# Reloading stored sums between transposing loads, and moving four additions behind the last sums, at the end of a gated feed-forward kernel

## The chip, the core and the metric

The kernel runs on one core of one Trainium2 chip. The metric is the device time of one execution in microseconds (us). The kernel before took 540.11 us as the median of three runs (540.02 to 540.7). The profile comes from one further execution, which took 539.99 us; its span from the first to the last instruction is 538.2 us, so 1.79 us lie around the span. The engines are PE (matrix products), DVE (elementwise, two inputs), ACT (copies, casts, the gelu), POOL (elementwise) and SP, which here only issues DMAs. ACT issues a few DMAs too.

## The reference

```python
def reference(x, w_gate, w_up, w_down):      # x 1x2048x1024, w_gate and w_up 1024x3584, w_down 3584x1024, bf16
    g = jnp.einsum("bsd,df->bsf", x, w_gate)
    u = jnp.einsum("bsd,df->bsf", x, w_up)
    h = _gelu(g) * u
    return jnp.einsum("bsf,fd->bsd", h, w_down)
```

## The kernel before, in words

The 2048 rows are taken in two passes of 1024 rows, each of two halves of 512 rows. In each pass the gate and up products run first, with h left in the on-chip memory, and then the down product (function `down`). All three products use Strassen's scheme in Winograd's form: a 2x2 block product is made of seven products of sums of blocks instead of eight, and the blocks of the result are sums of these products. In `down` the four blocks of the result ("quadrants" of the pass) are two halves of the rows by two halves of the columns.

In the second pass `down` goes one level deeper for one of its products (function `apart`): its result comes out transposed, as 16-bit planes written to DRAM (`pt0` to `pt3`), and is read back with transposing DMA loads. This concerns two quadrants, which the code numbers 0 and 1: quadrant 0 is read back by eight transposing loads issued from ACT, quadrant 1 by eight issued from SP (`turn_back`, the DMA at line 745). Two loads, n and n + 4, make one piece of 128 rows; there are four pieces for each quadrant. ACT puts the planes of a piece together into 32-bit numbers (`join`, line 750, 128x1024 16-bit elements).

What is then done with them, line by line:

- Quadrant 0 completes four pieces of the **first pass's** output. For these the sums of the first pass had been stored to DRAM (`ud`, line 949). `fetch_u3(i)` reloads the sum of piece i (line 757, 128x512 32-bit, 256 KB, a DMA on SP's queue). `put_0(i)` joins piece i of quadrant 0 on ACT into a buffer `gt`, adds the reloaded sum on DVE (line 121, the helper through which every DVE operation is recorded, output `st`), and stores the result (line 850, on SP's queue).
- Quadrant 1 completes four pieces of the second pass. `join_1(i)` joins piece i on ACT into the buffer `turned[1]`, which the end of `down` adds to four finished banks of products (line 946).

The last stretch of `down` (lines 937 to 957) makes what the code calls the products 7 and 3. For t from 0 to 13 one step is taken from the agenda, and then four matmuls of product 7 (`rows(e, q73[t][0], ...)`) are issued; with a lag of three steps six of the fourteen quadruples of product 3 run between them, and the other 32 matmuls at the very end, ordered by piece, with a final addition and store after each piece. The operands of step t are made by `make73(j)`: three DVE operations of 128x512 (outputs `q`, lines 670 to 672: `s3`, `t3` for product 7, and `s4` for product 3) and one cast on ACT (`tb`, line 677 for j below 8 and line 133 from 8 on). "Last sums" in the change's name are the ones that `make73` makes for j = 10 to 13.

In the second `down` the order on every engine is that in which the code calls the operations (`manual_schedule` holds all five engines there). The agenda is a table by step: `at(last, step, what, *args)` enters a call, `step()` makes the calls entered for the current step, in the order in which they were entered. Steps 66 to 79 are the fourteen turns of t in the last stretch. `make73(10)` to `make73(13)` stand at the steps 70, 71, 72 and 73 and come first in their steps, since they were entered earlier. SP works through its DMAs in the order of issue; an issue that has to wait holds all later ones.

Buffers for `u3`, `gt`, `q`, `tb`, `st` come from one pool of 36 slots (`kpool`): a new tile takes over a slot whose last reader has to be done. Moving a call therefore changes which slot each later tile gets, and so the waits.

Of the kernel before, what the change touches and what calls it, by code (L numbers as in the profile page):

```python
# [10 lines left out]
def kernel(  # L11
# [794 lines left out]
    def at(last, step, what, *args):  # L806
        agenda.setdefault((last, int(step)), []).append((what, args))
# [24 lines left out]
        at(1, 52 + n // 2, turn_back, 0, n)  # L832
        at(1, 59 + n, turn_back, 1, n)
    for i in range(NS):
        at(1, 66 + i, fetch_u3, i)
        at(1, (70, 72, 74, 76)[i], put_0, i)
        at(1, (71, 73, 75, 77)[i], join_1, i)
    moves = [(c, ko) for ko in range(KH) for c in range(2)]
    moves += [(c, ko) for c in (1, 0) for ko in range(KH, NKB)]
    sa = {}  # L840
# [483 lines left out]
```

## Time and profile before

| what | value |
| --- | --- |
| median of three runs | 540.11 us (540.02 to 540.7) |
| profiled execution, its span | 539.99 us, 538.2 us |
| PE busy | 529.5 us, 98% of the span |
| DVE busy | 404.0 us, 75% |
| ACT busy | 302.2 us, 56% |
| POOL busy | 268.3 us, 50% |
| granted PE clock | 1.0 in every slice |
| last PE matmul ends, last DVE operation ends | 534.75 us, 535.47 us |
| PE busy from 520 to 539 us of the span | 10.94 of 19 us |

All times within the profile are microseconds from the start of the span. In the timeline a row is: start, duration, engine, line, operation, output<-input, number of instructions merged; in square brackets the idle time of the engine ahead of the row and what ended it. `u<-ud` is the reload of a stored sum, `w<-pt` a transposing load, `gt<-w` the join of quadrant 0, `w<-w` at line 750 the join of quadrant 1, `st<-gt,u` the addition of `put_0`, `st<-bank,...` the final additions. "SPq" stands for the issuing of DMAs on SP. The chain of work that ended last is followed back from the last instruction, at each step to what released it.

### The profile page before, as it was taken

The page shows a single profiled execution, that of the slowest core. Times are in us where ns is not written, and L with a number is a line of the kernel's source. Part 1 is how long each engine was busy: PE and PEld are TensorE (multiplying, and loading weights), DVE is VectorE, ACT ScalarE, POOL GpSimd, SP SyncE. Part 2 cuts the span into 40 slices and gives each one's busy share as a digit, 9 for nine tenths or more (in the row PEclk, how much of TensorE's full clock was granted, in tenths as well). Part 3 has the DMA queues.
Part 4 walks back from the last instruction along what each step waited for, and adds up shares of the span by engine and source line. Part 5 has one row for each costly group of instructions (what it writes and reads, how often), then busy time and mean ns, then how long its engine had stood idle before and what let it go on. Part 6 is the DMA issues. An engine that isn't in the chain of part 4 may idle for free.

```text
span 538.2 us, 7762 instructions
## 1 busy us (share of the span) xinstructions
PE 529.5 (98%) x2375; PEld 374.2 (70%) x2375; DVE 404.0 (75%) x645; ACT 302.2 (56%) x544; POOL 268.3 (50%) x259
## 2 busy tenths in 40 slices
PE   9999999999999999999999999999999999999986
PEld 5568686868676774688877686866767764778754
DVE  2988768787777786749699887658576599789837
ACT  2557686868586841015576776666666621181742
POOL 1179977979797960000004989694896700000000
PEclk9999999999999999999999999999999999999999
DMA  9795218685777699999897999947363599599854
GB/s 244 162 240 174 80 60 292 197 293 197 234 233 247 205 377 381 369 316 246 227 293 215 302 315 355 250 117 197 88 186 118 198 362 345 160 319 320 182 129 146
DMA packets 141161, 126.09 MB, mean 234 GB/s; under 512 B 31680, under 2 KB 119232, under 8 KB 141120
## 3 DMA queue, kind: packets, MB, share of 16 engines
q1 hardware_dynamic: 136768, 124.55, 75.5%
q10 hardware_dynamic: 4352, 1.05, 1.1%
q8 instruction: 19, 0.31, 0.2%
q14 instruction: 22, 0.18, 0.1%
HBM read 86.38 MB, written 31.06 MB: 218 GB/s over the span
## 4 chain that ended last, share of the span: by engine, by line
PE 91%; DVE 3%; SPq 3%; DMA 1%; issue 1%; ACT 1%; DVEq 0%; ACTq 0%
PE bank L145 91%; DVE q L121 2%; SPq L745 2%; DMA w<-in_w_up_dram 1%; DVE xT L121 1%; DMA u<-ud 1%; ACT s L875 0%; SPq L995 0%; SPq L757 0%; DVE st L121 0%; ACT u L138 0%; SPq L662 0%; SPq L1014 0%; DVEq L121 0%; ACTq L138 0%
## 5 line engine op out<-in xcount | busy, mean ns | idle before, releaser
L124 POOL TENSOR_TENSOR s<-w 128x512 fp32r<-128x512 bf16 x102 | 117.5, 1170 | 49.6 <-DMA w<-in_w_gate_dram 35.5
L145 PE MATMUL bank<-t,s 128*128 128x512 f32 x528 | 126.3, 392 | 0.0
L145 PEld LDWEIGHTS bank<-t,s 128*128 128x128 f32 x528 | 99.1, 188 | 21.6 <-POOL s L124 0.3
L145 PE MATMUL bank<-xT,w 128*128 128x512 bf16 (+1 forms) x504 | 110.4, 376 | 0.1
L145 PEld LDWEIGHTS <-w 128*128 128x128 bf16 x504 | 47.7, 98 | 58.3 <-issue 4.2
L213 ACT ACTIVATE g<-sum 128x512 f32<-128x512 f32 x81 | 51.5, 636 | 59.8 <-DVE sum L121 57.8
L138 ACT COPY p<-bank 128x512 f32<-128x512 f32 x98 | 55.1, 590 | 47.3 <-PE bank L145 47.3
L121 DVE TENSOR_TENSOR hT<-g,bank 128x512 bf16<-128x512 f32 x72 | 48.9, 687 | 18.0 <-ACT g L213 12.4
L145 PE MATMUL bank<-q 128*128 128x512 f32 x224 | 57.4, 394 | 4.1 <-DVE q L121 3.9
L124 POOL TENSOR_TENSOR s<-w,s 128x512 fp32r<-128x512 bf16 x50 | 57.8, 1174 | 0.4
L124 POOL TENSOR_TENSOR s<-s,w 128x512 fp32r<-128x512 f32 x50 | 57.4, 1168 | 0.2
L121 DVE TENSOR_TENSOR bank<-bank,p 128x512 f32<-128x512 f32 x74 | 51.3, 695 | 5.9 <-PE bank L145 5.3
L145 PE MATMUL bank<-t,sa 128*128 128x512 f32 x216 | 54.9, 397 | 0.0
L145 PE MATMUL bank<-tb,s 128*128 128x512 f32 x216 | 54.3, 394 | 0.0
L199 POOL COPY seen<-t 128x1 f32<-128x1 f32 x2 | 0.4, 184 | 107.2 <-DVE t L121 107.2
L145 PEld LDWEIGHTS bank<-q 128*128 128x128 f32 x224 | 41.8, 188 | 15.0 <-DVE q L121 5.7
L145 PEld LDWEIGHTS bank<-t,sa 128*128 128x128 f32 x216 | 40.6, 188 | 9.1
L145 PEld LDWEIGHTS bank<-tb,s 128*128 128x128 f32 x216 | 40.5, 188 | 9.0 <-POOL s L124 0.3
L121 DVE TENSOR_TENSOR sum<-bank,p 128x512 f32<-128x512 f32 x54 | 37.0, 685 | 12.8 <-PE bank L145 11.7
L138 ACT COPY u<-bank 128x512 f32<-128x512 f32 x62 | 35.4, 595 | 17.4 <-PE bank L145 13.7
L133 ACT CAST tb<-raw 128x512 fp32r<-128x512 bf16 x20 | 12.4, 627 | 36.5 <-DMA raw<-in_w_down_dram 30.1
L133 ACT CAST sa<-w 128x512 fp32r<-128x512 bf16 x54 | 30.7, 616 | 2.7 <-DMA out_dram<-st 2.7
(121 smaller groups left out, 733.2 us busy)
## 6 DMA issues: line engine op xcount, KB each, us to landing
raw<-in_w_down_dram SPq DMA_DIRECT2D x72, 256.0 KB, 5.5
w<-in_w_gate_dram SPq DMA_DIRECT2D x27, 512.0 KB, 4.6
w<-in_w_up_dram SPq DMA_DIRECT2D x27, 512.0 KB, 5.9
td<-m SPq DMA_DIRECT2D x11, 768.0 KB, 5.3
q<-td SPq DMA_DIRECT2D x28, 256.0 KB, 5.2
pd<-xT SPq DMA_DIRECT2D x10, 512.0 KB, 5.7
w<-td SPq DMA_DIRECT2D x5, 1024.0 KB, 7.7
p<-pd SPq DMA_DIRECT2D x20, 256.0 KB, 4.8
```

The source lines that it names most:

```text
L121: nc.vector.tensor_tensor(out=out, in0=a, in1=b, op=op)
L124: nc.gpsimd.tensor_tensor(out=out, in0=a, in1=b, op=op)
L133: nc.scalar.copy(out=t, in_=src)
L138: nc.scalar.copy(out=t, in_=ps)
L145: nc.tensor.matmul(ps, lhsT=lhs, rhs=rhs, start=start, stop=stop, skip_group_check=True)
L199: nc.gpsimd.tensor_copy(out=seen, in_=tile[:, :1].bitcast(f32))
L213: nc.scalar.activation(g, src, ACT.Gelu_apprx_tanh)
L745: queue.dma_start_transpose(out=turned["tp", quad][:, i, half], in_=pt[2 * quad + half][:, i * P : (i + 1) * P])
```

## The change

```diff
     for n in range(2 * NS):
         at(1, 52 + n // 2, turn_back, 0, n)
         at(1, 59 + n, turn_back, 1, n)
     for i in range(NS):
-        at(1, 66 + i, fetch_u3, i)
-        at(1, (70, 72, 74, 76)[i], put_0, i)
-        at(1, (71, 73, 75, 77)[i], join_1, i)
+        at(1, 61 + i, fetch_u3, i)
+        at(1, 75 + i, put_0, i)
+        at(1, 71 + i, join_1, i)
```

NS is 4. No operation is added or removed. On SP's queue the four reloads move from behind the eighth transposing load of quadrant 1 to the places behind its third, fourth, fifth and sixth. On ACT the four joins of quadrant 1, which alternated with those of quadrant 0, come first, between the casts of `make73(11)` to `make73(13)` and behind them, and the four joins of quadrant 0 follow as the last work of ACT. On DVE the four additions of `put_0`, of which one stood behind `make73(10)`, one behind `make73(12)` and two behind `make73(13)`, all stand behind `make73(13)`, ahead of the final additions to the banks. PE's and POOL's orders are the same. The slots that `u3`, `gt` and the later `q` and `tb` tiles take over are other ones.

## The prediction

> **What bounds the kernel now.** I read the chain of work that ended last first, since PE's 98% is a mean over the span. PE holds it until the last 35 us; from there it leaves PE.
>
> ```profile
> 511.82 1.26 SPq L745
> 513.13 2.06 SPq L745
> 515.23 1.26 SPq L745
> 516.59 0.52 SPq L757
> 518.15 3.13 DMA u<-ud
> ...
> 526.22 8.54 PE bank L145 x36
> 534.78 0.69 DVE st L121
> ```
>
> SP's row of transposing loads, then the reloads, then DVE's sums, then PE, then the last addition, which ends at 535.47. The timeline of DVE and of PE tells what stands behind this:
>
> ```profile
> 508.82 0.69 DVE L121 TENSOR_TENSOR q<-hL,q 128x512 fp32r<-128x512 bf16 x1
> 520.06 0.69 DVE L121 TENSOR_TENSOR st<-gt,u 128x512 bf16<-128x512 f32 x1 [10.56 <-DMA u<-ud]
> 520.67 0.68 DVE L121 TENSOR_TENSOR q<-hT 128x512 fp32r<-128x512 bf16 x1
> ```
>
> ```profile
> 517.96 1.99 PE L145 MATMUL bank<-q 128*128 128x512 f32 x8
> 522.01 1.20 PE L145 MATMUL bank<-q 128*128 128x512 f32 x4 [2.07 <-DVE q L121]
> 523.81 1.21 PE L145 MATMUL bank<-q 128*128 128x512 f32 x4 [0.60 <-DVE q L121]
> 526.22 1.20 PE L145 MATMUL bank<-q 128*128 128x512 f32 x4 [1.19 <-DVE q L121]
> ```
>
> DVE stands 10.56 us on the first addition of put_0, whose reload is the ninth DMA behind the transposing loads. The nine sums of make73(11) to make73(13) are queued behind it, and PE starts the last three quadruples of product 7 late. Three waits, 3.86 us in all; by starts it is more. A quadruple takes 0.93 us when nothing waits (516.10 to 517.02), so the eight matmuls at 517.96 would be followed at 519.82. The real starts are 522.01, 523.81, 526.22 and 527.25: lost are 2.19 + 0.87 + 1.48 + 0.10 = **4.64 us**. That is all that can be had here.
>
> **The change, part by part.**
>
> *DVE's wait goes.* Behind 508.82 the nine sums follow at DVE's pace of 0.60 us. Owing to the other slots, one sum of make73(9) waits in the changed program for a product 7 matmul that ends at 507.9 instead of for one three quadruples earlier; that puts DVE back by 0.9 us. The sums end near 508.82 + 0.69 + 0.9 + 9 x 0.60 = 515.8. PE needs the first of them at 519.82, so it has 4 us of cover, and PE's last matmul ends at 534.76 - 4.64 = 530.1. I found no other new wait on DVE or PE that comes later than its engine's own work.
>
> *SP's row gets longer.* The eight transposing loads begin at 503.49, 506.74, 507.92, 509.22, 510.52, 511.82, 513.13 and 515.23; the first reload now stands behind the third. A reload behind a transposing load costs SP 0.52 us and 0.10 of semaphore and gaps (516.49 to 517.11, plus 0.05); a transposing load behind a copy took 1.14 and 1.16 instead of 1.26 (503.49, 506.74). So each of the four reloads adds about 0.55. Without the one long issue (2.06 instead of 1.26 at 513.13) the eighth began at 514.4; with four reloads at 516.6, with a long issue again at 517.4. The buffers of the reloads cost no wait: the matmuls and the sum that they wait for ended by 501.7. Queued behind the first reload are five transposing loads, behind the last two, and then only the output stores, which cannot start before 522.
>
> *When the eighth has landed.* Every load of quadrant 1 has these times to landing, and issue times beside them:
>
> ```profile
> L745 SPq DMA_TRANSPOSE w<-pt x8: 1136/1258/2062, 503.5 to 515.2; - x8
> DMA to landing us min/median/max: 2.6/4.6/6.3
> ```
>
> The second row spans both queues; SP's eight alone have a median of 2.7 and a longest of 4.2, those issued from ACT beside heavy loading 5.9. A transposing load with a 256 KB reload 1.2 us ahead of it is not in this stretch; the bounds are 2.6 and 6.0. I take 3.1, nearest to SP's own rows, since the seventh stands between the last reload and the eighth. The eighth has landed at 516.6 + 3.1 = **519.7**, 1.8 us later than now (515.23 + 2.7 = 517.9).
>
> *ACT and DVE behind it.* This is what is late next. In the changed order the join of piece 3 of quadrant 1 waits for the eighth load, and the four joins of quadrant 0, whose data has lain ready since about 503, stand behind it. A join follows a join after 1.065 us and takes 1.16: the last ends at 519.7 + 4 x 1.065 + 1.16 = 525.1. DVE's fourth addition starts there; twelve final additions follow, at 0.60 each, as they ran in
>
> ```profile
> 530.29 2.47 DVE L121 TENSOR_TENSOR st<-bank,w 128x512 bf16<-128x512 f32 x4
> ```
>
> The last starts at 525.15 + 12 x 0.60 = 532.35 and takes 0.69: **533.04**. PE, done at 530.1, would allow 530.8; so the end passes from PE to the chain SP, landing, ACT, DVE, and 2.2 of the 4.64 us are given back. Each 1 us by which the eighth load lands later moves the end by 1 us; at 522.1 nothing is won.
>
> *The stores.* Sixteen stores follow DVE at 0.60 us; SP issues one in 0.33, landing 1.7. The 2.73 us from the last addition to the end of the span stay.
>
> **Sum.** 535.47 - 533.04 = 2.43 us off 539.99 gives 537.56; the median of the runs lies 0.12 above the profiled execution, so 537.7.
>
> **A rule to weigh.** The reloads put 1 MB of reads among the transposing loads. The Trainium skill, "DMA: Bandwidth & Descriptors", section "Latency and other measured facts", gives the memory's access latency as 0.2 us on average and 2 us at high load. If that is the state they make, each landing is 1.8 us longer than SP's 2.7, an estimate from that page: the eighth lands at 521.1 and the sum is 539.1. The trace has both: 2.7 alone, 5.9 beside other loads at a DMA share above 1.0; the share here, from 507 to 519, is 0.41 to 0.82.
>
> **Rivals.**
>
> 1. *PE stays the bound.* If SP issues the reloads in the gaps (DMA share 0.33 at 510 to 512) and the eighth lands by 517.5, the additions are through when PE is: 530.83 instead of 535.47, so 535.5. For it: without the long issue the eighth would begin at 514.4 and need 2.6. Against it: each reload has a measured 0.37 to 0.52 of issue on the same queue. 0.06.
>
> 2. *Crowding.* The transposing loads land with the median of all sixteen, 4.6, not 3.1: end 1.5 later, 539.2; with the 5.9 of ACT's, 540.5. For it: the load issued at 511.82 took 4.2 with nothing but transposing loads about, and a stretch of 512 to 514 shows a DMA share of 0.91 at 128 GB/s. Against: a reload of 262144 bytes each 1.9 us (one reload and one transposing load on SP) is 138 GB/s, against 349 at 519 to 521, where the reloads run alone. 0.14.
>
> 3. *Slower: the queue changes between copies and transposing loads one after the other.* If a load of one kind starts only when the last of the other kind has landed, eight changes lie between the third load of quadrant 1 and the seventh. At 2.7 and 3.3 us each (the landings of a transposing load and of a reload) this puts the eighth at 536 and the time at 554. The place is SP's row; slower than now begins at a landing of 522.1, slower by over 0.2% at 523.3, that is at 0.45 us for each change. For it: nothing shows such a close mix here. Against: the four 128 KB weight loads issued right behind the first transposing load landed in 2.3 to 2.7, and the second, issued 0.06 after the last of them, in 2.8, so two changes cost nothing; in the first pass two transposing loads between copies (268.52, 271.74) landed in 4.3 and 3.1. At a mild 0.6 for each change the time is 542.5. 0.08. The Trainium skill, same page, "Rules for kernel authors", says that a transpose next to ordinary DMAs needs nothing; by that, this rival falls.
>
> That the change does not do what it says (a reload held by its buffer, so that SP stands) has no support: their last readers are done at least 7 us before.
>
> **How the numbers follow.** Forecast 537.7 with 0.72 (its own range, landing 2.6 to 4.0 with and without a long issue: 537.2 to 538.9). A change of under 0.2%, 1.1 us, is about what a measurement of this kernel can't tell from none. Faster than 539.0: 0.72 + 0.06 + 0.04 of crowding = 0.82. Within 0.2%: 0.10. Slower: 0.08. The range 536.4 to 539.6 leaves out the PE bound below, and above it the slower rival and the upper part of crowding, 0.18 in all.
>
> **What would show it.** Right: no idle of DVE ahead of a st<-gt,u with releaser "DMA u<-ud" of 10 us; PE without gaps from 484 to 530; idle ahead of ACT's w<-w joins with releaser "DMA w<-pt"; the four gt joins last on ACT, ending near 525; DVE without a gap for the final twelve additions and the chain's end through ACT and SP instead of PE. Wrong: a PE wait on q behind 518; a transposing load between reloads that lands after 4 us or more or whose issue takes over 2 us; a last addition that waits for PE, which would mean rival 1.

## The result, and the profile after

| | before | after |
| --- | --- | --- |
| median of ten runs each | 541.28 us (539.02 to 542.89) | 539.06 us (538.75 to 540.3) |
| ratio after / before | | 0.9967 (95% interval 0.9951 to 0.9983) |
| a second measurement, 12 runs against 28 | 542.02 us | 540.16 us, ratio 0.9965 (0.9948 to 0.9983) |
| profiled execution, its span | 539.99, 538.2 us | 540.3, 538.5 us |

The change gains 0.33%, 1.8 us, with an interval of 0.9 to 2.7; the ratio is that of the means, and the medians lie 2.2 us apart. The forecast was 2.43 us, a ratio of 0.9955, and a time of 537.7 us, which none of the ten runs reached.

The two spans don't show this gain: they begin the last stretch at different times. The first transposing load of quadrant 1 ("the first load" below) is issued at 503.49 in the profile before and at 504.41 after. I therefore count from the first load. The last addition ends 31.98 us behind it before, 31.37 after; another profile of each gives 31.75 (first load at 505.54) and 30.95 (504.82). So the stage itself gains 0.4 to 1.0 us, where 2.43 were forecast.

SP's row after the change, from the timeline (start, duration):

```profile
510.19 0.52 SPq L757 DMA_DIRECT2D u<-ud  x1
510.75 1.12 SPq L745 DMA_TRANSPOSE w<-pt  x1
...
513.77 1.58 SPq L757 DMA_DIRECT2D u<-ud  x1
515.39 1.12 SPq L745 DMA_TRANSPOSE w<-pt  x1
516.61 0.52 SPq L757 DMA_DIRECT2D u<-ud  x1
517.18 2.43 SPq L745 DMA_TRANSPOSE w<-pt  x2
```

A reload costs 0.52 and the transposing load behind it 1.12, as forecast; one issue is long again (1.58). What these loads set in motion is seen on ACT and on DVE:

```profile
517.32 1.17 ACT L750 COPY w<-w 128x1024 uint16<-128x1024 uint16 x1 [6.52 <-DMA w<-pt]
518.39 0.62 ACT L133 CAST tb<-raw 128x512 fp32r<-128x512 bf16 x1
518.97 1.17 ACT L750 COPY w<-w 128x1024 uint16<-128x1024 uint16 x1
520.05 0.61 ACT L133 CAST tb<-raw 128x512 fp32r<-128x512 bf16 x1
521.34 2.24 ACT L750 COPY w<-w 128x1024 uint16<-128x1024 uint16 x2 [0.68 <-DMA w<-pt]
523.49 4.39 ACT L750 COPY gt<-w 128x1024 uint16<-128x1024 uint16 x4
```

```profile
515.96 0.68 DVE L121 TENSOR_TENSOR q<-hL,q 128x512 fp32r<-128x512 bf16 x1
524.69 0.69 DVE L121 TENSOR_TENSOR st<-gt,u 128x512 bf16<-128x512 f32 x1 [8.05 <-ACT gt L750]
...
535.10 0.68 DVE L121 TENSOR_TENSOR st<-bank,u 128x512 bf16<-128x512 f32 x1
```

The 10.56 us of waiting ahead of DVE's sums are gone: the sums now run through and end at 516.64. DVE still stands for 9.2 us, 8.05 and then three times 0.4, but later, and on ACT's joins of quadrant 0 instead of a reload. ACT begins with the joins of quadrant 1 at 517.32, when the fifth load lands (issued at 512.55, landed in 4.7), and the last of them starts 18.0 us behind the first load, where the forecast says 16.2. PE runs product 7 without a gap:

```profile
517.82 1.10 PE L145 MATMUL bank<-xT,q 128*128 128x512 f32 x4
518.75 4.71 PE L145 MATMUL bank<-q 128*128 128x512 f32 x20
```

The chain that ended last no longer goes through PE at its end:

```profile
517.18 4.14 DMA w<-pt
...
523.58 4.31 ACT gt L750 x4
...
528.52 2.48 DVE st L121 x4
...
531.60 4.18 DVE st L121 x7
```

The seventh load's landing (4.14 us), ACT, DVE: the passage that was forecast, 1.8 us later than forecast.

Landings of SP's eight transposing loads, in us from the start of the issue; the reloads stand ahead of loads 4 to 7 in the changed kernel and in `e11`. Two of the rows are of kernels that start with more warm-up matmuls (`e8`, `e11`); they are explained with their experiments.

| kernel | 1 | 2 | 3 | 4 | 5 | 6 | 7 | 8 |
| --- | --- | --- | --- | --- | --- | --- | --- | --- |
| before | 2.6 | 2.8 | 2.8 | 2.7 | 2.7 | 4.2 | 3.6 | 2.7 |
| after | 2.7 | 2.8 | 2.7 | 3.9 | 4.7 | 3.6 | 4.1 | 3.5 |
| after, second profile (`e5_after_again`) | 3.3 | 2.6 | 2.7 | 3.7 | 4.9 | 4.2 | 3.4 | 2.9 |
| `e1_late_adds` | 2.5 | 2.7 | 2.7 | 2.7 | 4.5 | 3.9 | 3.3 | 2.6 |
| `e8_shifted_program` | 2.4 | 3.5 | 2.7 | 2.5 | 2.6 | 2.7 | 2.6 | 2.8 |
| `e11_after_shifted` | 3.6 | 3.3 | 2.8 | 3.9 | 4.0 | 3.9 | 4.1 | 3.4 |

### The profile page after: what moved, and what is told of

The parts are those of the page before. It is cut to its first block, busy times and chain, and to the rows that moved or that the text cites. A ratio compares the mean times of both kernels' runs of the same rounds, so it can differ in the third digit from the quotient of the medians.

```text
span 538.5 us, 7762 instructions
## 1 busy us (share of the span) xinstructions
PE 528.5 (98%) x2375; PEld 374.9 (70%) x2375; DVE 404.4 (75%) x645; ACT 302.0 (56%) x544; POOL 268.4 (50%) x259
## 4 chain that ended last, share of the span: by engine, by line
PE 89%; DMA 4%; DVE 3%; ACT 2%; issue 1%; SPq 0%; ACTq 0%; DVEq 0%
PE bank L145 88%; DMA w<-pt 2%; DVE q L121 2%; DVE st L121 1%; DMA raw<-in_w_down_dram 1%; ACT gt L750 1%; DMA q<-td 1%; PE bank L1057 1%; PE bank L1002 1%; ACT s L875 0%; ACT xT L733 0%; SPq L662 0%; DVE xT L121 0%; ACTq L1319 0%; ACT u L138 0%
## 5 line engine op out<-in xcount | busy, mean ns | idle before, releaser
L121 DVE TENSOR_TENSOR hT<-g,bank 128x512 bf16<-128x512 f32 x72 | 49.0, 687 | 17.6 <-ACT g L213 11.9
L133 ACT CAST tb<-raw 128x512 fp32r<-128x512 bf16 x20 | 12.3, 624 | 37.3 <-DMA raw<-in_w_down_dram 29.0
```

Source lines behind the costliest of these rows:

```text
L121: nc.vector.tensor_tensor(out=out, in0=a, in1=b, op=op)
L133: nc.scalar.copy(out=t, in_=src)
```

## The experiments

**Theory A**: the reloads among the transposing loads make quadrant 1 late, and the second part of the change, which puts all of ACT's and DVE's ready work behind quadrant 1, exposes that. **Rival B**: the reloads cost nothing there; the joins are late for a reason that both kernels share. **Rival C**: the late additions are of use only with the early reloads.

In every diff the minus lines are the changed kernel's. All times in the stage are in us, counted from the first load of that kernel's own profile. That is the right zero where the chain to the end runs through these loads. Where PE is the bound (`e4`, `e10`) it is not quite: in the kernels with 7 warm-up matmuls in which no sum holds PE, PE's last matmul ends 25.3 to 26.9 us behind the first load, so these two compare with the others only to within about 1.5 us. All rows but the first two are of one profile each:

| kernel | last join of quadrant 1 starts | last addition ends | ratio to before |
| --- | --- | --- | --- |
| before, two profiles | 23.15, 22.93 | 31.98, 31.75 | |
| after, two profiles | 18.00, 17.58 | 31.37, 30.95 | 0.9967, 0.9965 |
| `e1_late_adds` | 15.77 | 29.12 | 0.9898 (0.9869 to 0.9927) |
| `e2_early_reloads` | 21.10 | 29.09 | 0.9923 (0.9896 to 0.995) |
| `e3_reloads_ahead` | 15.56 | 28.93 | 0.9917 (0.9888 to 0.9947) |
| `e4_adds_in_gap` | 15.52 | 26.30 | 0.9872 (0.9845 to 0.99) |
| `e6_split_reloads` | 19.15 | 32.51 | 0.9999 (0.9979 to 1.002) |
| `e7_half_reloads` | 16.5 | 29.94 | 0.9936 (0.9913 to 0.9959) |
| `e8_shifted_program` | 14.24 | 27.61 | one execution |
| `e10_joins_in_gap` | 14.53 | 27.12 | 0.9904 (0.9877 to 0.9932) |
| `e11_after_shifted` | 17.62 | 31.00 | one execution |
| `e12_half_shift` | 14.34 | 27.70 | one execution |

### The second part alone: e1_late_adds

```diff
-        at(1, 61 + i, fetch_u3, i)
+        at(1, 66 + i, fetch_u3, i)
```

> Only the second part of the change: the additions and joins of quadrant 0 late as in the changed kernel, the four reloads behind the eighth transposing load as before. Theory A (the reloads among the transposing loads delay the joins of quadrant 1, and with them the end): the eighth load is issued 11.7 us behind the first and the last join of quadrant 1 starts 14.5 us behind it instead of 18.0; the last addition ends 27.9 us behind the first load instead of 31.4, so the time is about 3.5 us below the changed kernel, 4 us below the kernel before. Rival B (the reloads cost the row nothing; the changed kernel fell short because its execution lost time ahead of the changed part, and the row of transposing loads is as slow without them): last addition again 31 us behind the first load, time within 0.7 us of the changed kernel. Rival C (the late additions need the reloads early): DVE waits for a reload behind the joins, last addition later than 31.4.

The reloads go back behind the eighth load, the additions stay late. SP and ACT:

```profile
506.03 9.51 SPq L745 DMA_TRANSPOSE w<-pt  x7
515.64 1.95 SPq L757 DMA_DIRECT2D u<-ud  x4
```

```profile
514.30 1.17 ACT L750 COPY w<-w 128x1024 uint16<-128x1024 uint16 x1 [6.16 <-DMA w<-pt]
...
517.49 2.23 ACT L750 COPY w<-w 128x1024 uint16<-128x1024 uint16 x2
519.62 4.39 ACT L750 COPY gt<-w 128x1024 uint16<-128x1024 uint16 x4
```

The first join starts 11.5 us behind the first load instead of 12.9, no later join waits, and the reloads, issued last, are there before ACT has made `gt`. The stage is 1.8 to 2.2 us shorter than with both parts. Rivals B and C fall. The end is later than theory A had it, since the fifth load still took 4.5 us; `e8` and `e12` look into that.

### The first part alone: e2_early_reloads

```diff
-        at(1, 75 + i, put_0, i)
-        at(1, 71 + i, join_1, i)
+        at(1, (70, 72, 74, 76)[i], put_0, i)
+        at(1, (71, 73, 75, 77)[i], join_1, i)
```

> Only the first part of the change: the four reloads among the transposing loads, the additions and joins of quadrant 0 where they were before, alternating with those of quadrant 1. Theory A: the transposing loads land as late as in the changed kernel (fifth 12.9 us, seventh 16.9 us behind the first), but two joins of quadrant 0 are done before and between those of quadrant 1, so the last join starts about 20.5 us behind the first load with no other join behind it; DVE has done all four additions of put_0 by 21.2 and ends 28.4 behind the first load: 3 us below the changed kernel. Rival B: nothing to gain from the order of the joins, within 0.7 us of the changed kernel. Rival C (the second part was needed to free DVE): make73(13) stands behind an addition that waits for a join, PE waits on q by 1 us or more, slower than the changed kernel.

DVE, with the additions where they were before:

```profile
514.42 0.69 DVE L121 TENSOR_TENSOR st<-gt,u 128x512 bf16<-128x512 f32 x1 [2.26 <-DMA u<-ud]
...
521.34 0.69 DVE L121 TENSOR_TENSOR st<-gt,u 128x512 bf16<-128x512 f32 x1 [2.62 <-ACT gt L750]
...
526.14 0.69 DVE L121 TENSOR_TENSOR st<-gt,u 128x512 bf16<-128x512 f32 x1 [1.44 <-ACT gt L750]
```

Of the 10.56 us of waiting 2.26 are left, and PE waits for none of the sums. The transposing loads behind reloads land as late as in the changed kernel (loads 4 to 8: 3.6, 5.4, 4.7, 3.4, 3.0), but the joins of quadrant 0 alternate with those of quadrant 1 and fill ACT's time between landings: its last join begins at 526.02 with nothing behind it, and the end is 29.09. **Either part alone takes away the wait that PE felt, and each alone gains about 2 us more in the stage than both.**

### Reloads ahead of all transposing loads: e3_reloads_ahead

```diff
-        at(1, 61 + i, fetch_u3, i)
+        at(1, 58, fetch_u3, i)
```

> The changed kernel with its four reloads ahead of the first transposing load of quadrant 1 (agenda step 58 instead of 61 to 64), where SP stands idle for 3 us; joins and additions as in the changed kernel. Theory A: the row of transposing loads is as short as before (eighth issued 11.7 us behind the first), the last join of quadrant 1 starts 14.5 us behind the first load; the first load itself comes 0 to 1 us later; time 2.5 to 3.5 us below the changed kernel. Rival B: time within 0.7 us of the changed kernel.

```profile
499.63 3.67 SPq L757 DMA_DIRECT2D u<-ud  x4
504.72 1.16 SPq L745 DMA_TRANSPOSE w<-pt  x1
507.97 9.29 SPq L745 DMA_TRANSPOSE w<-pt  x7
```

With the reloads ahead, on SP's free time, the row of loads is as short as in `e1`, and so is the stage (28.93). It is the reloads' place among the loads that costs, not that they are made.

### Ready work into ACT's wait: e4_adds_in_gap

```diff
-        at(1, 61 + i, fetch_u3, i)
-        at(1, 75 + i, put_0, i)
-        at(1, 71 + i, join_1, i)
+        at(1, 58, fetch_u3, i)
+        at(1, 71 + i // 2, put_0, i)
+        at(1, 74 + i, join_1, i)
```

> Reloads ahead of the first transposing load as in the run before, and the four joins and additions of quadrant 0 in the gap that ACT and DVE have behind the sums of make73(11) and make73(12) (agenda steps 71 and 72), the joins of quadrant 1 last. Theory A and the arithmetic of the prediction's first rival: nothing but the joins of quadrant 1 hangs on the transposing loads, the last of them ends by 20 us behind the first load, PE is the bound, and DVE's last addition follows PE's last matmul at once: 4.6 us below the kernel before, 3.5 to 5 below the changed kernel, at best 0.6 below the first two of these runs. Rival B: the row of transposing loads holds the end in this order too, not below the changed kernel by more than 2 us.

```profile
513.74 1.28 DVE L121 TENSOR_TENSOR st<-gt,u 128x512 bf16<-128x512 f32 x2
...
522.73 1.89 DVE L121 TENSOR_TENSOR st<-bank,m 128x512 bf16<-128x512 f32 x3 [2.89 <-PE bank L145]
...
530.74 0.69 DVE L121 TENSOR_TENSOR st<-bank,u 128x512 bf16<-128x512 f32 x1 [1.14 <-PE bank L145]
```

Joins and additions of quadrant 0 run while ACT and DVE would stand, the joins of quadrant 1 come last, and DVE waits for PE twice: PE is the bound again. The stage is the shortest, and the ratio the lowest, 0.9872, though its interval overlaps those of `e1` and `e10`.

### The changed kernel and the one before once more: e5_after_again, e9_before_again

No edit.

> The changed kernel itself, for a second profile of it and for a measurement beside the same runs of the kernel before as the three runs that follow. Theory A (each reload among the transposing loads delays the later ones): last join of quadrant 1 starts 17.5 to 18.5 us, last addition ends 31.0 to 31.8 us behind the first transposing load of quadrant 1, as in the first profile (18.0 and 31.4). Rival B (the first profile was an execution disturbed ahead of the change): nearer to the forecast's 16.2 and 29.6.

> The kernel before itself, for a second profile. The first had the first transposing load of quadrant 1 at 503.5 us and its last addition 32.0 us behind it, in an execution of 539.99, while most executions took 541 to 543. If the executions differ ahead of the changed part: first load at 504 to 507 and the last addition again 31.5 to 32.5 behind it. If they differ in the changed part: first load near 503.5 and the last addition 33 to 35 behind it, by the long issues and late landings of the transposing loads or a later reload.

The stage repeats within 0.4 us (30.95 and 31.37; 31.75 and 31.98). In `e9` DVE waits 10.41 us where it waited 10.56, and the first load comes at 505.54 us instead of 503.49: the two executions of the kernel before differ ahead of the changed part. In the second profile after, the fifth load took 4.9 us, and the five operations of ACT behind it, 4.26 us, set the start of the last join without a further wait:

```profile
518.14 1.17 ACT L750 COPY w<-w 128x1024 uint16<-128x1024 uint16 x1 [6.46 <-DMA w<-pt]
...
521.33 2.23 ACT L750 COPY w<-w 128x1024 uint16<-128x1024 uint16 x2
```

### Issue or bytes: e6_split_reloads, e7_half_reloads

```diff
-        nc.sync.dma_start(out=turned["u3", i], in_=ud[:, i])
+        for c0 in (0, N // 2):
+            nc.sync.dma_start(
+                out=turned["u3", i][:, c0 : c0 + N // 2], in_=ud[:, i, c0 : c0 + N // 2]
+            )
```

> The changed kernel with each reload issued as two DMAs of half the columns: the same bytes, twice the issues. If what a reload costs is its issue on SP (0.5 us each): the eighth transposing load is issued 16 us behind the first instead of 13.9, the last addition ends 33.4 behind it instead of 31.4, 2 us slower than the changed kernel. If it is the bytes among the transposing loads: 31.4, no slower by more than 0.5 us.

```diff
-        turned["u3", i] = slot([P, N], f32, "u3")
-        nc.sync.dma_start(out=turned["u3", i], in_=ud[:, i])
+        turned["u3", i] = slot([P, N // 2], f32, "u3")
+        nc.sync.dma_start(out=turned["u3", i], in_=ud[:, i, : N // 2])
...
```

The rest of this edit is in `put_0`, which adds the half to both halves.

> The changed kernel reloading only the first half of the columns of each stored sum and adding it to both halves (the second half of each reload is left out): the same issues, half the bytes. If the cost is the issue: eighth load issued 13.9 us behind the first, last addition 31.0 to 31.6. If it is the bytes: the loads behind a reload land in 3 us instead of 3.9 to 4.7, the last join of quadrant 1 starts 1 us earlier and the last addition ends at 30.3.

Twice the issues for the same bytes put the end at 32.51, 1.1 to 1.6 later than in the changed kernel. Half the bytes with the same issues put it at 29.94, 1.0 to 1.4 earlier. The runs measured beside each other order the three the same way: medians of 541.43, 540.16 and 538.33 us for `e6`, the changed kernel and `e7`. So both count. The four reloads and the loads 4 to 8 of the changed kernel and then of `e7`, with KB each and the median time to landing:

```profile
u<-ud SPq DMA_DIRECT2D x4, 256.0 KB, 4.3
w<-pt SPq DMA_TRANSPOSE x5, 3.9
```

```profile
u<-ud SPq DMA_DIRECT2D x4, 128.0 KB, 2.6
w<-pt SPq DMA_TRANSPOSE x5, 2.6
```

In the median these loads land in their usual 2.6 us with 128 KB ahead, and in 3.9 with 256 KB.

### Why e1 and e3 end 1 us late: e8_shifted_program, e12_half_shift, e11_after_shifted

In every profile so far one 16 KB packet of the queue that the page of the profile calls "instruction" starts between 512 and 516 us. In `e1` it starts at 512.25: the late loads are the fifth to the seventh, which are in flight while it runs, and the one long issue (1.82 us) begins at 512.42. The stretch from 509 to 515 us of `e1` (packets, MB and share of the DMA engines' time in the first row):

```profile
q8 instruction: 1, 0.02, 1.0%
issues: line engine op xcount, KB each, median us to landing
w<-pt SPq DMA_TRANSPOSE x5, 3.3
```

Adding warm-up matmuls at the kernel's start leaves the packet at about the same time from the span's start and moves the work, and so the loads, behind it. `e8` and `e12` do this to `e1`, `e11` to the changed kernel.

```diff
-    NWARM = 7
+    NWARM = 31
```

> The kernel of the first run of the study (additions late, reloads behind the eighth load) with 31 instead of 7 warm-up matmuls at the start, which moves PE's instruction fetches (one of 16 KB for each 128 matmuls, by their count) 5.6 us earlier against the rest; the whole execution is longer by those matmuls. In five profiles one such fetch at 512 to 514 was followed by transposing loads that landed in 4.2 to 4.7 us instead of 2.7 and by one issue of 1.6 to 2.2 us instead of 1.26. If the fetch is the cause: that spell comes 5.6 us earlier, among the first three loads, and the fourth to eighth land in 2.7 and are issued in 1.26; the fifth lands 9.8 us behind the first load instead of 11.5 and the last addition ends 27.9 to 28.3 behind it instead of 29.1. If not: the spell stays 8 to 12 us behind the first load.

In `e8` the first load starts at 509.10 and the packet at 512.55, on the second load and the weight loads ahead of it:

```profile
q8 instruction: 1, 0.02, 3.9%
issues: line engine op xcount, KB each, median us to landing
raw<-in_w_down_dram SPq DMA_DIRECT2D x1, 128.0 KB, 3.3
w<-pt SPq DMA_TRANSPOSE x1, 3.5
```

The spell has moved with it: the second load lands in 3.5, loads 4 to 8 in 2.5 to 2.8. The stage ends at 27.61, near the 27.9 that theory A had for `e1`.

> The kernel of the first run of the study with 19 instead of 7 warm-up matmuls: PE's instruction fetch falls 2.8 us earlier against the row, half as far as in the run with 31. If the fetch causes the spell of late landings: it moves to the third and fourth load (issued 4.4 and 5.7 us behind the first), which land in 3.5 to 4.5, with the long issue at the fifth or sixth, and the loads from the sixth on land in 2.5 to 2.8; the last addition ends 27.6 to 28.8 us behind the first load. If the place of the spell with 31 was chance: fourth load 2.7, fifth 4.2 to 4.5 as in four profiles with 7.

`e12` has 19 warm-up matmuls. I missed the place: the first load came at 508.61, only half a microsecond earlier than in `e8`, so the packet again met the second load (3.4; the others 2.4 to 2.8). The end, 27.70, was as expected. That the spell moves with the packet is shown at two places, not at three; that the packet is its cause is argued from this, since no run here is without it.

> The changed kernel with 31 instead of 7 warm-up matmuls at the start, so that PE's instruction fetch falls 5.6 us earlier against the row of transposing loads (the whole execution is longer by the matmuls). If the late landings of the fifth to seventh load in the changed kernel come from the fetch: they land in 2.7 to 3.0, as without reloads, the last join of quadrant 1 starts 15.5 us behind the first load and the last addition ends 28.9 behind it. If from the reloads alone: 3.5 to 4.9 again, 17.6 to 18.0 and 31.0 to 31.4. If both add up: 3.3 to 3.7 behind each reload, eighth load issued 13.1 behind the first, last join at 16.2 to 16.8, last addition at 29.5 to 30.2.

In `e11` the packet falls at 511.63, ahead of the second load. The stretch of 517 to 526 us holds no such packet, and the loads behind reloads land late all the same:

```profile
u<-ud SPq DMA_DIRECT2D x4, 256.0 KB, 4.0
w<-pt SPq DMA_TRANSPOSE x5, 3.9
```

The last join starts at 17.62 and the end is 31.00. So the reloads alone are enough to make the loads late. They may not be the whole of it: the fifth load, in flight with the packet in the two profiles after, took 4.7 and 4.9 us there and 4.0 here. Nor is it shown that the stage gains nothing, since in `e11` the second load is issued 3.92 us behind the first instead of 3.25 and 3.46.

### Only the joins early: e10_joins_in_gap

```diff
-        at(1, 61 + i, fetch_u3, i)
+        at(1, 71 + i // 2, join_0, i)
+        at(1, 66 + i, fetch_u3, i)
...
-        at(1, 71 + i, join_1, i)
+        at(1, 74 + i, join_1, i)
```

`join_0` is the join out of `put_0`; the addition stays at 75 + i.

> The four reloads behind the eighth transposing load as in the kernel before, the joins of quadrant 0 on ACT in the gap ahead of those of quadrant 1 (agenda steps 71 and 72; they need no reload), the four additions on DVE behind make73(13) as in the changed kernel. Theory A: the row of transposing loads is as short as in the first run of the study, ACT's last join is over about 17 us behind the first load, the last reload lands 18.6 behind it, DVE could end at 26.5 and PE is the bound: DVE's last addition ends 0.7 us behind PE's last matmul, time as in the fourth run (4 to 7 us below the kernel before) or up to 1 us better, since no reloads run beside the loads of quadrant 0. Rival: the reloads land late enough to hold DVE, last addition more than 2 us behind PE's last matmul, no better than the first run.

```profile
521.24 0.69 DVE L121 TENSOR_TENSOR st<-gt,u 128x512 bf16<-128x512 f32 x1 [4.08 <-DMA u<-ud]
...
531.78 0.69 DVE L121 TENSOR_TENSOR st<-bank,u 128x512 bf16<-128x512 f32 x1 [0.61 <-PE bank L145]
```

With ACT's ready joins in its gap the reloads may stay behind the eighth load: they are late for DVE by 4.08 us, but the last addition waits for PE. In the stage it ends at 27.12, against 29.12 for `e1`; by the runs' intervals (0.9904 and 0.9898) the two can't be told apart. Against `e4` the 0.8 us lie in the place of the first load: in both the last addition ends 0.7 us behind PE's last matmul.

## Why the prediction was right and wrong

- **DVE's wait goes; PE runs through**: right. The sums end 12.2 us behind the first load (forecast 12.3), and all three PE waits are gone. PE's last matmul ends at 530.79, 26.4 behind the first load (forecast 26.6).
- **SP's row**: right. The eighth load is issued 13.93 and 13.19 us behind the first in the two profiles; the forecast was 13.1, or 13.9 "with a long issue again". I took the first, and the long issue came in one of the two.
- **"When the eighth has landed" with "I take 3.1"**: this is the step that failed. The prediction let the last join wait for the eighth load alone, and gave no price to the loads directly behind a reload, the fourth to the seventh. These took 3.4 to 4.9 us, and one of them decided, with ACT's row behind it: the seventh (4.1) and one join in the first profile, the fifth (4.9) and five operations of ACT in the other. So the last join started at 18.0 and 17.6 instead of 16.2. In the second profile all of this is the path: the eighth load had landed at 16.1, in 2.9 us. In the first, 0.8 us are the long issue, 0.4 the eighth's landing of 3.5, and 0.5 the seventh load. Of the 2.43 us, 0.4 to 1.0 were left in the stage. The prediction had named this sign of being wrong: "a transposing load between reloads that lands after 4 us or more".
- **Its range**: a landing of 4.0 together with a long issue gives 537.7 + 0.9 + 0.8 = 539.4 by the prediction's own terms, not the 538.9 at which its own range stops. The measured median, 539.06, lies between the two.
- **The tail**: right. From the start of the last join to the end of the last addition 13.37 us (forecast 13.34), from there to the end of the span 2.7.
- **Rivals**: PE did not stay the bound. A change of the queue between kinds did not drain it: eight changes, no landing over 4.9 us in the changed kernel, and 13.93 for the whole row. Crowding, at 0.14, came nearest: its landing of 4.6 puts the last addition 31.05 us behind the first load and the time at 539.2; measured were 31.37 and 30.95, and 539.06. Since it too had the eighth load decide, the closeness is in part luck. For it the prediction cited a load that took 4.2 "with nothing but transposing loads about"; but an instruction packet (see `e8`) started at 512.89, while that load was in flight.
- **The rule that was weighed**: the Trainium skill's page "DMA: Bandwidth & Descriptors" gives under "Latency and other measured facts" 0.2 us for an access to the memory on average and 2 us at high load. The direction fits, 2.7 us alone and 3.4 to 4.9 behind reloads, and the 1.8 us more lies in the upper half of what was seen (0.7 to 2.2); that the memory's latency is the cause no run shows. The DMA shares that the prediction sets against it, 0.41 to 0.82, are those of windows of 2 us from 507 on; in windows from 508 on the same stretch has 0.33 and 0.91. The Trainium skill's "Rules for kernel authors" on that page say that a transpose next to ordinary DMAs needs nothing. Nothing drained here, but such a neighbour is not free: 1.3 us in the median (3.9 against the 2.6 of `e7`).
- **What stays open.** The stage gained 0.4 to 1.0 us, the runs 1.8 (0.9 to 2.7), and `e1` to `e4` also gain about 1 to 3 us more in the runs than against the stage before (`e4` 6.9 us, where the prediction calls 4.64 all that can be had). The first load itself comes at 502.8 to 506.8 us in the profiles of the kernels with 7 warm-up matmuls, and PE waits at 499 to 500 for a reload in some of them and not in others:

```profile
499.37 1.16 PE L145 MATMUL bank<-q 128*128 128x512 f32 x4 [1.43 <-DMA q<-td]
```

The row is of the changed kernel; `e9` has 1.96 us there, the first profile before none. So the sign "PE without gaps from 484 to 530" did not hold there. The change stands behind this place in every order, so I ascribe none of it to the change; one or two profiles per kernel can't tell whether the slots that it moves have a part in it.

The granted clock bears on this. In all the profiles it stands at 1.00 until PE's last matmul and falls only behind it (after: 1.00 from 531 to 535 us, 0.59 from there to the end), and both profiles of the kernel before have 1.000 in the mean. Of the 52 executions of that kernel that were timed beside the experiments, only 9 have 1.000, and took 540.7 us in the mean; 33 have 0.993 or 0.994 and took 542.6. So most executions before are not like the two whose stage is shown here, while those of the changed kernel (0.995 to 0.998) are like its profiles (0.997). Where the others lose their 2 us, and what the change does to that, stays open, since no trace of one was kept.

## What to carry to other kernels

When an in-order engine stands on a late load, one may ask for the load earlier or put the waiting work later. Price both alone and together: here each took the wait away by itself, and together they gave about 2 us of the stage back, since the earlier asking delayed the queue's next loads, and the work that was put later had filled just the time of that delay. Shortest was a third order: ready work in the gaps where its engine stands, reloads ahead of the crowded row, and behind the latest landing only what needs it.

## What the runs showed of the hardware

A transposing load issued 0.6 us behind a 256 KB copy landed in 3.4 to 5.4 us instead of 2.7 (the changed kernel twice, `e2` and `e11`), though the DMA engines moved only 159 GB/s in that stretch (510 to 519 us of the first profile after, busy share 0.82), far from the 349 at which the reloads ran alone before. Behind 128 KB it landed in 2.5 to 3.3 (`e7`).

A single 16 KB instruction packet (19 in a run, for 4750 matmul and weight-load instructions, about one for 250) falls into this stage in each of the 14 profiles. One to three of the transposing loads in flight with it, where no reload is near, landed in 3.0 to 4.5 us, and in 13 of the 14 one DMA issue that begins within 0.8 us of the packet took 0.3 to 1.1 us longer than its like (1.5 to 2.2 us instead of 1.1 or 1.26 where it was a transposing load's). With more matmuls at the start of PE's program the packet meets other loads.
